# Pooled attention and two expert layers on one core: the first token block's layers in three float32r products instead of plain float32

## The chip, the cores and the metric

The kernel runs on one NeuronCore of a Trainium2 chip. The metric is the time of one execution on the device in microseconds (us). The engines are named as in the profile: PE is TensorE (PEld its weight loads), DVE is VectorE, ACT is ScalarE, POOL is GpSimd, SP is the queue that issues all DMAs of this kernel.

## The reference

Inputs are q, k and v (8 batches, 8 heads, 576 tokens, 64 features, float32), and the matrices w_a, w_b, w_out of a first layer and w_in, w_out of a second, which come as float64.

```python
k_p = k.reshape(B, H, Sp, pool, D).mean(axis=3)      # pool = 8, Sp = 72
v_p = v.reshape(B, H, Sp, pool, D).mean(axis=3)
scores = scale * np.matmul(q, k_p.transpose(0, 1, 3, 2))
...                                                  # softmax over the 72 pooled keys
x = np.matmul(attn, v_p)                             # 4608 tokens x 512
y = (x @ w_a) * (x @ w_b) @ w_out                    # 512 -> 1536 -> 512
h = y @ w_in                                         # 512 -> 2048
out = (h * np.clip(h + 3.0, 0.0, 6.0) / 6.0) @ w_out2
```

## The kernel before

The 4608 tokens are cut into nine blocks of 512. For each block j, attention gives x (512 features in four groups of 128 partitions, by 512 tokens), and the first layer runs over twelve slices f of 128 hidden features. `step(j, f)` (L646) issues for a slice: the product pa of x with a slice of w_a, the product pb with a slice of w_b, their elementwise product g, and, one step late (`pend`), `y_part` (L513), which adds w_out times g to the four accumulators of the block. At the end of a block y goes to DRAM. After all blocks the second layer runs over the whole of y; the change does not touch it.

**Two ways of multiplying.** From block 1 on, each operand is split into a float32r high half and a float32r low half (`split`, L72: the high half is a rounding copy, by default on ScalarE; the low half is a subtraction, by default on GpSimd), and a product takes three matmuls, high by high, low by high and high by low (`mm3`, L495; recorded at L497, L498 and L499). In block 0 x, the weights and g are left whole, and the products are plain float32 (L505 and L519).

**The decode.** The weights are float64, read as pairs of 32-bit words, and each tile (128 by 512 weights, 512 KB, named st) is turned into float32 in block 0, in three stages: `decode_begin` (two operations on ScalarE, L79 and L80), `decode` (two on VectorE, L85 and L86, and an add on GpSimd, L87) and `decode_end` (one on VectorE, L91). A slice f has three tiles, part 0 (w_a), 1 (w_b) and 2 (w_out), numbered n = 3 f + part. A step is cut into three slots, s = 3 f, 3 f + 1 and 3 f + 2 in block 0; `run_slot(s)` issues the attention work that is planned for the slot, `w1_slot(s)` (L468) issues begin of tile s + 4, end of tile s + 2 and mid of tile s + 3. Everything is issued in the order of the program (`manual_schedule`), and each engine works through its own instructions in order.

**The splits of the weights.** They are made from the last step of block 0 on, one step ahead: `wa_split` (L474) of the w_a slice, whose tile then stays in SBUF for all later blocks, and `raw_split` (L484) of the other two, which are also stored to DRAM (`w1dram`) in the next step. From block 2 on, `w1_load` reads these two back three steps ahead. Staged, raw, split and loaded tiles share the 28 buffers of `wpool`.

**The plan of the attention.** The tokens of a block fall into chunks of up to 128. `plan` gives every piece of work of a chunk a slot: q transposed (`q_tr`), scores, exponential (`expo`), sums, normalisation (`normal`, three operations on GpSimd, L296, L303, L309), transposes of the attention (`at_main`, `at_left`), the product with v (`pv`, which also writes x into `xh`, and from block 1 on the low half into `xl`, L360). For a new batch, k and v are summed over 8 (`sum8`, L132 to L134), and their loads are issued some slots earlier (`dma_at`, L406), into four buffers of the pool `ld` for batches 1 and 2.

**The prelude** (L576) does this for block 0 by a list written by hand. It loads k of the first head pair, q of chunk 0, the other k, q of chunk 1, v, the last rows of v (`vl`), q of chunks 2 and 3 and the first nine weight tiles. `sc(c)` transposes q of a chunk and takes its scores at once.

```python
        def sc(c):
            q_tr(c)
            scores(c, 0)
            scores(c, 1)
```

Of the kernel before, what the change touches and what calls it, by code (L numbers as in the profile page):

```python
# [15 lines left out]

# [9 lines left out]
def pooled_attention_then_two_moe_kernel(  # L26
# [79 lines left out]
    def x_tiles(j):  # L106
        if j not in xh_t:
            xh_t[j] = xpool.tile([P, NCC, TB], F32R if j else F32, tag="xh", name=f"xh{j}")
            xl_t[j] = xpool.tile([P, NCC, TB], F32R, tag="xl", name=f"xl{j}") if j else None
        return xh_t[j], xl_t[j]  # L110
# [77 lines left out]
    def vl_prep(b):  # L188
        t = vlraw.pop(b)
        vs = a2.tile([96, 2, D], F32, tag="kv", name="vls", bufs=3)  # L190
        sum8(vs, t)
        vpool[b, 2] = vs
# [152 lines left out]
    def pv(pi, g):  # L345
        b, t0, N = pieces[pi]
        ath, atl, atx = aT[pi]
        pt = ps.tile([P, 2, PIECE], F32, tag="att", name="pv")
        for i in range(2):
            hp = 2 * g + i  # L350
            o = pt[:, i, :N]
            nc.tensor.matmul(o, vmh[b % 2][:, hp], ath[:, hp, :N], start=True, stop=False)
            nc.tensor.matmul(o, vml[b % 2][:, hp], ath[:, hp, :N], start=False, stop=False)
            nc.tensor.matmul(o, vlw[b % 2][:96, hp], atx[:, g, :N], start=False, stop=False)
            nc.tensor.matmul(o, vmh[b % 2][:, hp], atl[:, hp, :N], start=False, stop=True)
        j, r = divmod(b * S + t0, TB)
        xh, xl = (x[:, 2 * g : 2 * g + 2, r : r + N] if x is not None else x for x in x_tiles(j))
# [80 lines left out]
    wa_t, raw_t, rawa_t, w1st, wst = {}, {}, {}, {}, {}  # L438
# [10 lines left out]

    def w1_begin(n):  # L450

        f, part = divmod(n, 3)
        if part == 0:
            raw_t[f] = wpool.tile([P, 2, 512], F32, tag="w", name=f"raw{f}")
            if f % 2 == 0:
                rawa_t[f] = wpool.tile([P, 2, 512], F32, tag="w", name=f"rawa{f}")
            else:
                rawa_t[f] = rawa_t[f - 1]
        wst[n] = raw_t[f][:, part - 1] if part else rawa_t[f][:, f % 2], w1st[f][part]
        decode_begin(*wst[n])  # L460
# [4 lines left out]
    def w1_end(n):  # L465
        decode_end(*wst.pop(n))
# [7 lines left out]
    def wa_split(f):  # L474
        w = wpool.tile([P, 2, 512], F32R, tag="w", name=f"wa{f}")
        split(w[:, 0], w[:, 1], rawa_t[f][:, f % 2], lo_eng=nc.vector)
        wa_t[f] = w
# [5 lines left out]

    def raw_split(key, f, part):  # L484
        w = wpool.tile([P, 2, 512], F32R, tag="w", name=f"sp{key}_{part}")
        split(w[:, 0], w[:, 1], raw_t[f][:, part], lo_eng=nc.vector if part else nc.gpsimd)
        later.append((w1dram[f][part], w.bitcast(F32)))
        sp_t[key, part] = w
# [12 lines left out]
    def layer_in(o, w, xh, xl):  # L501
        for c in range(NCC):
            s = slice(c * P, (c + 1) * P)
            if xl is None:
                nc.tensor.matmul(o, w[:, s], xh[:, c], start=c == 0, stop=c == NCC - 1)  # L505
                continue
# [6 lines left out]
    def y_part(j, f, w, gh, gl):  # L513
        if f == 0:
            yacc[j] = [ps_acc.tile([P, TB], F32, tag="acc", name=f"y{c}") for c in range(NCC)]
        for c in range(NCC):
            s = slice(c * P, (c + 1) * P)
            if gl is None:
                nc.tensor.matmul(yacc[j][c], w[:, s], gh, start=f == 0, stop=f == NF1 - 1)  # L519
                continue  # L520
# [55 lines left out]
    def prelude():  # L576

        k_dma(0, 0)
        q_dma(0)
        for hp in range(1, NP):  # L580
            k_dma(0, hp)
# [3 lines left out]
        vl_dma(0)  # L585
        q_dma(2)
        q_dma(3)
        for f in range(3):
            w1_dma(f)
# [4 lines left out]
        def sc(c):  # L594
            q_tr(c)
            scores(c, 0)
            scores(c, 1)
# [4 lines left out]

        sc(0)
# [3 lines left out]
        sums(0)  # L607
        v_prep(0, 1)
        expo(1)
        normal(0)  # L610
        v_write(0, 0)
        sums(1)
        sc(2)
        w1_begin(0)
        normal(1)
        at_chunk(0)
        expo(2)
        vl_prep(0)
        v_write(0, 1)
        sums(2)  # L620
        w1_mid(0)
        sc(3)
        normal(2)
        expo(3)
        vl_split(0)
        at_chunk(1)
        w1_begin(1)
        w1_end(0)
        sums(3)
# [12 lines left out]
        w1_begin(3)
# [3 lines left out]
    def step(j, f):  # L646
# [11 lines left out]
        nj, nf = divmod(NF1 * j + f + 1, NF1)  # L658
# [10 lines left out]
        layer_in(pa, wa_t[f] if j else rawa_t[f][:, f % 2], xh, xl)  # L669
# [60 lines left out]
    t = 0  # L730
# [228 lines left out]
```

## Time and profile before

| | us |
|---|---|
| median of three runs | 1855.4 |
| lowest and highest | 1855.19, 1856.17 |
| the profiled execution | 1853.53 |
| its span | 1851.7 |

The profile is of one execution. Times in it count from the start of the span. A row of a timeline gives start, duration, engine, line, operation, output and input; a row of groups gives line, engine, operation, output and input, shapes and count, then the busy time and the mean duration in ns, then the idle time of the engine just before and what ended it. Matmuls overlap in the records, so the price of one is read from start to start.

### The profile page before, as it was taken

The numbers are of one execution on the slowest core, as the hardware profiler recorded it, in microseconds if no ns is written. First come the engines' busy times: TensorE is split into PE (matmuls) and PEld (weight loads), VectorE is DVE, ScalarE is ACT, GpSimd is POOL, SyncE is SP. The second block draws the span as 40 slices with busy tenths as digits, with TensorE's granted clock in tenths as the row PEclk, the third lists the DMA queues.
The fourth block names the chain that finished last, engine by engine and source line by source line (L and its number), as shares of the span: only waits on it lengthen the run. The fifth ranks groups of instructions, "written<-read, shape, count | busy, mean of one in ns | idle before, by whom it ended". The sixth has DMA issues, their size and how long they took to land.

```text
span 1851.7 us, 23399 instructions
## 1 busy us (share of the span) xinstructions
PE 1796.2 (97%) x8148; PEld 1438.6 (78%) x8148; DVE 947.3 (51%) x1609; ACT 726.9 (39%) x1389; POOL 763.0 (41%) x661
## 2 busy tenths in 40 slices
PE   4999999999999999999999989999999999999998
PEld 3444788888888788888888777888888888888897
DVE  6687655323444445444322336676557445644645
ACT  3544443323333333333333335444334433533443
POOL 3454454333443444444343575554225222422322
PEclk8999999999999999999999999999999999999999
DMA  9552346635746547565545465546445544644483
GB/s 250 174 161 50 115 145 214 217 109 154 247 150 195 199 150 229 183 210 185 187 160 199 163 244 185 207 173 227 151 151 182 178 146 142 210 137 149 152 296 127
DMA packets 196549, 328.72 MB, mean 178 GB/s; under 512 B 86352, under 2 KB 107856, under 8 KB 196432
## 3 DMA queue, kind: packets, MB, share of 16 engines
q1 hardware_dynamic: 196432, 327.22, 53.5%
q8 instruction: 65, 1.06, 0.2%
q14 instruction: 52, 0.43, 0.1%
HBM read 264.24 MB, written 62.91 MB: 177 GB/s over the span
## 4 chain that ended last, share of the span: by engine, by line
PE 88%; DVE 5%; DMA 1%; ACT 1%; issue 1%; POOL 0%; SPq 0%; DVEq 0%; ACTq 0%; POOLq 0%
PE o L497 7%; PE o L499 7%; PE o L498 7%; PE y L497 5%; PE pb L497 5%; PE y L499 4%; PE pb L499 4%; PE y L498 4%; PE pb L498 4%; PE pa L497 4%; PE pa L499 4%; PE pa L498 4%; PE phZ L497 3%; PE phZ L498 3%; PE phZ L499 3%; PE sc L258 2%
## 5 line engine op out<-in xcount | busy, mean ns | idle before, releaser
L74 POOL TENSOR_TENSOR g<-r,g 128x512 fp32r<-128x512 f32 (+1 forms) x160 | 198.3, 1249 | 433.4 <-ACT g L73 263.8
L847 DVE TENSOR_TENSOR oacc<-o,oacc 128x512 f32<-128x512 f32 x252 | 172.2, 688 | 135.7 <-PE o L499 135.5
L498 PE MATMUL o<-wo,g 128*128 128x512 f32 x576 | 224.4, 390 | 0.0
L499 PE MATMUL o<-wo,g 128*128 128x512 f32 x576 | 224.2, 389 | 0.0
L689 POOL TENSOR_TENSOR asb<-asb,bsb 128x512 f32<-128x512 f32 x96 | 126.9, 1322 | 232.1 <-ACT bsb L684 206.8
L497 PE MATMUL o<-wo,g 128*128 128x512 f32 x576 | 211.6, 390 | 1.4 <-ACT g L73 1.2
L74 POOL TENSOR_TENSOR gl<-asb,gh 128x512 fp32r<-128x512 f32 x96 | 126.8, 1321 | 146.3 <-ACT gh L73 144.1
L671 ACT COPY asb<-pa 128x512 f32<-128x512 f32 x108 | 63.3, 586 | 243.0 <-PE pa L499 207.1
L497 PE MATMUL pa<-xh,wa 128*128 128x512 f32 x384 | 154.7, 403 | 0.0
L499 PE MATMUL pa<-xl,wa 128*128 128x512 f32 x384 | 150.2, 391 | 0.0
L498 PE MATMUL pa<-xh,wa 128*128 128x512 f32 x384 | 149.7, 390 | 0.0
L684 ACT COPY bsb<-pb 128x512 f32<-128x512 f32 x108 | 63.3, 586 | 192.4 <-PE pb L499 160.7
L828 ACT ACTIVATE r<-hs 128x512 f32<-128x512 f32 (+1 forms) x120 | 69.0, 590 | 164.7 <-DVE hs L878 163.8
L497 PEld LDWEIGHTS o<-wo,g 128*128 128x128 f32 x576 | 107.5, 188 | 23.8 <-ACT g L73 2.4
L499 PEld LDWEIGHTS o<-wo,g 128*128 128x128 f32 x576 | 108.1, 188 | 22.2
L498 PEld LDWEIGHTS o<-wo,g 128*128 128x128 f32 x576 | 108.2, 188 | 22.0
L73 ACT CAST g<-r 128x512 fp32r<-128x512 f32 (+1 forms) x160 | 91.9, 579 | 68.4 <-DVE r L829 68.2
L498 PE MATMUL phZ<-Sh,wi 128*128 128x512 f32 (+1 forms) x320 | 117.7, 368 | 0.0
L497 PE MATMUL phZ<-Sh,wi 128*128 128x512 f32 (+1 forms) x320 | 117.6, 368 | 0.0
L499 PE MATMUL phZ<-Sl,wi 128*128 128x512 f32 (+1 forms) x320 | 114.6, 368 | 0.0
L331 DVE TENSOR_TENSOR atl<-atm,ath 128x512 fp32r<-128x512 f32 (+1 forms) x40 | 25.5, 637 | 165.6 <-ACT ath L330 165.5
L829 DVE SCALAR_TENSOR_TENSOR r<-r,hs 128x512 f32<-128x512 f32 (+1 forms) x120 | 95.0, 808 | 26.5 <-ACT r L828 26.4
(1349 smaller groups left out, 4216.3 us busy)
## 6 DMA issues: line engine op xcount, KB each, us to landing
wi<-wsd SPq DMA_DIRECT2D x96, 512.0 KB
wo<-wod SPq DMA_DIRECT2D x64, 512.0 KB
wsd<-wi SPq DMA_DIRECT2D x24, 512.0 KB
kraw<-in_k_dram SPq DMA_DIRECT2D x32, 288.0 KB
ydram<-yo SPq DMA_DIRECT2D x36, 256.0 KB
out_dram<-oacc SPq DMA_DIRECT2D x36, 256.0 KB
vraw<-in_v_dram SPq DMA_DIRECT2D x32, 256.0 KB
w2st<-in_moe_w_in_dram SPq DMA_DIRECT2D x16, 512.0 KB
```

The source lines that it names most:

```text
L73: (hi_eng or nc.scalar.copy)(hi, src)
L74: (lo_eng or nc.gpsimd).tensor_tensor(lo, src, hi.bitcast(F32), ALU.subtract)
L258: nc.tensor.matmul(pt[:n, i * 2 * SP : (i + 1) * 2 * SP], qT[c][:, hp, :], bd[b % 2][hp], start=True, stop=True)
L497: nc.tensor.matmul(o, wh, xh, start=first, stop=False, skip_group_check=more)
L498: nc.tensor.matmul(o, wl, xh, start=False, stop=False, skip_group_check=more)
L499: nc.tensor.matmul(o, wh, xl, start=False, stop=last, skip_group_check=more)
L671: nc.scalar.copy(asb, pa)
L684: nc.scalar.copy(bsb, pb)
L689: nc.gpsimd.tensor_tensor(asb, asb, bsb, ALU.mult)
L828: nc.scalar.activation(r[:, :n], src, AF.Relu, bias=3.0)
L829: nc.vector.scalar_tensor_tensor(r[:, :n], r[:, :n], 6.0, src, ALU.min, ALU.mult)
L847: nc.vector.tensor_tensor(acc, o, acc, ALU.add)
```

## The change

Block 0 is computed like the others: x, weights and g are split, and every product takes three matmuls. Each tile of weights is decoded and split in block 0, one tile per slot: `w1_slot` now has four stages, begin of tile s + 5, mid of s + 4, end of s + 3 and split of s + 2; a stage may do two tiles in a slot until it has caught up, and takes only tiles that the stage before it had done when the slot began. High halves go to ScalarE, low halves to VectorE for parts 0 and 2 and to GpSimd for part 1. Parts 1 and 2 are stored to DRAM from block 0 on, and block 1 loads them, as the later blocks do. The splits in the last step of block 0 and in block 1 go away. The raw tiles come in pairs that are freed after the splits. In the prelude, all k are loaded before q of chunk 0, and the last rows of v after q of all chunks; q of a chunk is transposed about one chunk before its scores; the sum of those last rows moves from VectorE to GpSimd; tiles 0 and 1 are split. For batch 2, k is loaded three slots before its sum instead of six.

```diff
 def x_tiles(j):
-            xh_t[j] = xpool.tile([P, NCC, TB], F32R if j else F32, tag="xh", name=f"xh{j}")
-            xl_t[j] = xpool.tile([P, NCC, TB], F32R, tag="xl", name=f"xl{j}") if j else None
+            xh_t[j] = xpool.tile([P, NCC, TB], F32R, tag="xh", name=f"xh{j}")
+            xl_t[j] = xpool.tile([P, NCC, TB], F32R, tag="xl", name=f"xl{j}")
 def vl_prep(b):
-        sum8(vs, t)
+        sum8(vs, t, nc.vector if b else nc.gpsimd)
 def pv(pi, g):
         nc.scalar.copy(xh, pt[:, :, :N])
-        if j:
-            nc.vector.tensor_tensor(xl, pt[:, :, :N], xh.bitcast(F32), ALU.subtract)
+        nc.vector.tensor_tensor(xl, pt[:, :, :N], xh.bitcast(F32), ALU.subtract)
...
-            dma_at = [x - (6 if near else 8) for x in k_at], [x - (7 if near else 8) for x in v_at]
+            dma_at = [x - (3 if b == 2 else 6 if near else 8) for x in k_at], [x - (7 if near else 8) for x in v_at]
...
     def w1_begin(n):
...
+        if n % 2 == 0:
+            raw_t[0] = wpool.tile([P, 2, 512], F32, tag="w", name=f"raw{n}")
+        wst[n] = raw_t[0][:, n % 2], w1st[f][part]
         decode_begin(*wst[n])
...
+    def w1_split(n):
+        f, part = divmod(n, 3)
+        t, _ = wst.pop(n)
+        w = wpool.tile([P, 2, 512], F32R, tag="w", name=f"w1_{n}")
+        split(w[:, 0], w[:, 1], t, lo_eng=nc.gpsimd if part == 1 else nc.vector)
+        if part == 0:
+            wa_t[f] = w
+        else:
+            later.append((w1dram[f][part - 1], w.bitcast(F32)))
+            sp_t[(0, f), part - 1] = w
+
+    w1_done = [0] * 4
     def w1_slot(s):
-        for lead, fn in ((4, w1_begin), (2, w1_end), (3, w1_mid)):
-            if s + lead < 3 * NF1:
-                fn(s + lead)
+        limit = w1_done[1:] + [3 * NF1]
+        for i, (lead, fn) in enumerate(((2, w1_split), (3, w1_end), (4, w1_mid), (5, w1_begin))):
+            for _ in range(2):
+                if w1_done[i] <= s + lead and w1_done[i] < limit[i]:
+                    fn(w1_done[i])
+                    w1_done[i] += 1
...
 def prelude():
-        k_dma(0, 0)
+        for hp in range(NP):
+            k_dma(0, hp)
         q_dma(0)
-        for hp in range(1, NP):
-            k_dma(0, hp)
         q_dma(1)
         v_dma(0, 0)
         v_dma(0, 1)
-        vl_dma(0)
         q_dma(2)
         q_dma(3)
+        vl_dma(0)
...
 def step(j, f):
-        if nj == 1:
-            wa_split(nf)
-            raw_split((nj, nf), nf, 0)
-        if 2 <= lj < NB:
+        if 1 <= lj < NB:
             w1_load((lj, lf), lf, 0)
             w1_load((lj, lf), lf, 1)
...
-        if j == 0:
-            gh = gpool.tile([P, TB], F32, tag="gh", name="g0")
-            nc.gpsimd.tensor_tensor(gh, asb, bsb, ALU.mult)
-        else:
-            nc.gpsimd.tensor_tensor(asb, asb, bsb, ALU.mult)
+        nc.gpsimd.tensor_tensor(asb, asb, bsb, ALU.mult)
...
         gh = gpool.tile([P, TB], F32R, tag="gh", name="gh")
         gl = gpool.tile([P, TB], F32R, tag="gl", name="gl")
         split(gh, gl, asb)
```

## Rows read from the trace of the kernel before

**Rows 1.** The page: busy time of each engine over the span.

```profile
PE 1796.2 (97%) x8148; PEld 1438.6 (78%) x8148; DVE 947.3 (51%) x1609; ACT 726.9 (39%) x1389; POOL 763.0 (41%) x661
```

**Rows 2.** Stretches: from:to, length, busy per engine (instructions), PEclk, DMA share, GB/s.

```profile
10.00:49.60 39.60, 23.06 (x106) 20.10 (x107) 25.45 (x58) 16.85 (x39) 15.29 (x21) 0.74 1.02 274
49.60:194.30 144.70, 139.41 (x411) 67.02 (x410) 110.79 (x217) 69.12 (x140) 71.80 (x62) 0.98 0.42 119
194.30:208.20 13.90, 13.90 (x51) 8.54 (x50) 5.23 (x10) 5.27 (x10) 5.36 (x6) 1.00 0.26 102
208.20:330.00 121.80, 120.68 (x584) 100.30 (x584) 67.36 (x114) 53.24 (x109) 59.47 (x49) 1.00 0.54 178
```

**Rows 3.** Timeline of TensorE, in block 0 and in block 1.

```profile
162.69 3.60 PE L505 MATMUL pb<-xh,raw 128*128 128x512 f32 x8
166.12 3.60 PE L519 MATMUL y<-g,raw 128*128 128x512 f32 x8
...
172.41 0.38 PE L150 MATMUL ktp<-ident,kp 72*128 72x72 f32 x1 [1.61 <-DVE atl L331]
172.58 5.27 PE L505 MATMUL pa<-xh,rawa 128*128 128x512 f32 x8
...
218.96 0.39 PE L497 MATMUL pa<-xh,wa 128*128 128x512 f32 x1
...
221.68 0.39 PE L497 MATMUL pb<-xh,sp(1, 2)_0_1674 128*128 128x512 f32 x1
```

**Rows 4.** Groups of instructions: 49.6 to 194.3 us, the last over the whole span.

```profile
L87 POOL TENSOR_TENSOR raw<-raw,st 128x512 int32<-128x512 int32 x23 | 30.3, 1316 | 42.7 <-DVE raw L86 30.2 <-issue 10.4 <-DMA qraw<-in_q_dram 2.1
L87 POOL TENSOR_TENSOR rawa<-rawa,st 128x512 int32<-128x512 int32 x11 | 15.2, 1378 | 25.8 <-issue 12.1 <-ACT bsb L684 5.4 <-ACT st L80 4.1
L91 DVE SCALAR_TENSOR_TENSOR raw<-st,raw 128x512 uint32<-128x512 uint32 x23 | 18.8, 817 | 11.7 <-POOL raw L87 11.7
L91 DVE SCALAR_TENSOR_TENSOR rawa<-st,rawa 128x512 uint32<-128x512 uint32 x11 | 9.0, 814 | 0.5 <-POOL rawa L87 0.5
...
L74 POOL TENSOR_TENSOR gl<-asb,gh 128x512 fp32r<-128x512 f32 x96 | 126.8, 1321 | 146.3 <-ACT gh L73 144.1
```

**Rows 5.** Timeline of VectorE and of GpSimd at two places of block 0.

```profile
59.91 0.69 DVE L91 SCALAR_TENSOR_TENSOR raw<-st,raw 128x512 uint32<-128x512 uint32 x1 [2.91 <-POOL raw L87]
60.52 0.42 DVE L85 TENSOR_SCALAR raw<-raw 128x512 f32<-128x512 f32 x1
...
66.86 1.45 POOL L687 TENSOR_TENSOR g<-asb,bsb 128x512 f32<-128x512 f32 x1
67.29 1.17 DVE L134 TENSOR_TENSOR kp<-kraw 72x128 f32<-72x128 f32 x1
68.39 0.68 DVE L91 SCALAR_TENSOR_TENSOR rawa<-st,rawa 128x512 uint32<-128x512 uint32 x1
...
130.52 1.29 POOL L87 TENSOR_TENSOR rawa<-rawa,st 128x512 int32<-128x512 int32 x1 [3.27 <-ACT bsb L684]
131.78 1.26 POOL L687 TENSOR_TENSOR g<-asb,bsb 128x512 f32<-128x512 f32 x1
131.84 1.75 DVE L91 SCALAR_TENSOR_TENSOR rawa<-st,rawa 128x512 uint32<-128x512 uint32 x1 [0.48 <-POOL rawa L87]
133.01 1.48 POOL L296 TENSOR_TENSOR am<-sm,rc 128x512 f32<-128x512 f32 x1
133.52 1.26 DVE L85 TENSOR_SCALAR raw<-raw 128x512 f32<-128x512 f32 x1
```

**Rows 6.** Timeline of GpSimd in the prelude: the first and last of a normalisation's three operations.

```profile
39.45 1.04 POOL L296 TENSOR_TENSOR am<-sm,rc 128x512 f32<-128x512 f32 x1 [3.44 <-DVE rc L283]
...
40.83 0.34 POOL L309 COPY am<-ln 128x192 f32<-128x192 f32 x1
```

**Rows 7.** Waits of SP's queue up to 300 us: in total, times, longest.

```profile
SPq L223 <- DVE vs L134: 26.6, 1, 26.6
```

**Rows 8.** Groups of TensorE in the prelude, 0 to 49.6 us.

```profile
L258 PE MATMUL sc<-bd,qT 128*128 128x144 f32 x32 | 7.1, 382 | 6.9 <-ACT qT L241 6.9
```

More of the change, by code (lines that the diff above doesn't have):

```diff
@@ L356, in pv @@
         j, r = divmod(b * S + t0, TB)
-        xh, xl = (x[:, 2 * g : 2 * g + 2, r : r + N] if x is not None else x for x in x_tiles(j))
+        xh, xl = (x[:, 2 * g : 2 * g + 2, r : r + N] for x in x_tiles(j))
         nc.scalar.copy(xh, pt[:, :, :N])
-        if j:
-            nc.vector.tensor_tensor(xl, pt[:, :, :N], xh.bitcast(F32), ALU.subtract)
+        nc.vector.tensor_tensor(xl, pt[:, :, :N], xh.bitcast(F32), ALU.subtract)
     chunks, pieces, chunk_piece, block_chunks = [], [], {}, [[] for _ in range(NB)]
@@ L435, in run_slot @@
             fn(*args)
-    wa_t, raw_t, rawa_t, w1st, wst = {}, {}, {}, {}, {}
+    wa_t, raw_t, w1st, wst = {}, {}, {}, {}
     def w1_dma(f):
@@ L452, in w1_begin @@
         f, part = divmod(n, 3)
[L453 to L456, printed above, removed]
-            else:
-                rawa_t[f] = rawa_t[f - 1]
-        wst[n] = raw_t[f][:, part - 1] if part else rawa_t[f][:, f % 2], w1st[f][part]
+        if n % 2 == 0:
+            raw_t[0] = wpool.tile([P, 2, 512], F32, tag="w", name=f"raw{n}")
+        wst[n] = raw_t[0][:, n % 2], w1st[f][part]
         decode_begin(*wst[n])
@@ L465, in w1_end @@
     def w1_end(n):
-        decode_end(*wst.pop(n))
-    def w1_slot(s):
-        for lead, fn in ((4, w1_begin), (2, w1_end), (3, w1_mid)):
-            if s + lead < 3 * NF1:
-                fn(s + lead)
[L474 to L477, printed above, removed]
+        decode_end(*wst[n])
+    def w1_split(n):
[9 more added lines that the diff above has]
+    w1_done = [0] * 4
+    def w1_slot(s):
+        limit = w1_done[1:] + [3 * NF1]
[4 more added lines that the diff above has]
+                    w1_done[i] += 1
     sp_t = {}
@@ L482, in pooled_attention_then_two_moe_kernel @@
     w1dram = [[dpool.tile([P, 2, 512], F32, name=f"w1dram{f}_{i}") for i in range(2)] for f in range(NF1)]
[L484 to L488, printed above, removed]
     def w1_load(key, f, part):
@@ L503, in layer_in @@
             s = slice(c * P, (c + 1) * P)
-            if xl is None:
-                nc.tensor.matmul(o, w[:, s], xh[:, c], start=c == 0, stop=c == NCC - 1)
-                continue
             mm3(o, w[:, 0, s], w[:, 1, s], xh[:, c], xl[:, c], c == 0, c == NCC - 1)
@@ L517, in y_part @@
             s = slice(c * P, (c + 1) * P)
-            if gl is None:
-                nc.tensor.matmul(yacc[j][c], w[:, s], gh, start=f == 0, stop=f == NF1 - 1)
-                continue
             mm3(yacc[j][c], w[:, 0, s], w[:, 1, s], gh, gl, f == 0, f == NF1 - 1)
@@ L594, in sc @@
         def sc(c):
-            q_tr(c)
             scores(c, 0)
@@ L601, in at_chunk, with w1 @@
             at_left(c)
+        def w1(stage, n):
+            (w1_split, w1_end, w1_mid, w1_begin)[stage](n)
+            w1_done[stage] = n + 1
+        q_tr(0)
+        q_tr(1)
         sc(0)
@@ L607, in prelude @@
         sums(0)
+        q_tr(2)
+        expo(1)
         v_prep(0, 1)
-        expo(1)
         normal(0)
-        v_write(0, 0)
+        sc(2)
         sums(1)
-        sc(2)
-        w1_begin(0)
+        q_tr(3)
+        expo(2)
         normal(1)
         at_chunk(0)
-        expo(2)
+        v_write(0, 0)
+        sc(3)
+        sums(2)
+        expo(3)
         vl_prep(0)
+        w1(3, 0)
+        normal(2)
+        at_chunk(1)
         v_write(0, 1)
[L620 to L624, printed above, removed]
+        sums(3)
         vl_split(0)
[L626 to L629, printed above, removed]
+        w1(2, 0)
         vl_write(0)
         normal(3)
+        w1(3, 1)
         pv(0, 0)
         pv(0, 1)
+        w1(1, 0)
         at_chunk(2)
-        w1_mid(1)
-        w1_begin(2)
+        w1(2, 1)
+        w1(0, 0)
+        w1(3, 2)
         at_chunk(3)
-        w1_end(1)
+        w1(1, 1)
         pv(1, 0)
         pv(1, 1)
-        w1_mid(2)
-        w1_begin(3)
+        w1(2, 2)
+        w1(0, 1)
+        w1(3, 3)
         for x in sorted(x for x in plan if x < 0):
@@ L657, in step @@
                 w1_dma(f + 3)
-        nj, nf = divmod(NF1 * j + f + 1, NF1)
-        if nj == 1:
-            wa_split(nf)
-            raw_split((nj, nf), nf, 0)
         lj, lf = divmod(NF1 * j + f + AHEAD, NF1)
-        if 2 <= lj < NB:
+        if 1 <= lj < NB:
             w1_load((lj, lf), lf, 0)
@@ L668, in step @@
         pa = ps.tile([P, TB], F32, tag="ab", name="pa")
-        layer_in(pa, wa_t[f] if j else rawa_t[f][:, f % 2], xh, xl)
+        layer_in(pa, wa_t[f], xh, xl)
         asb = gpool.tile([P, TB], F32, tag="asb", name="asb", bufs=2)
@@ L681, in step @@
         pb = ps.tile([P, TB], F32, tag="ab", name="pb")
-        layer_in(pb, sp_t.pop(((j, f), 0)) if j else raw_t[f][:, 0], xh, xl)
+        layer_in(pb, sp_t.pop(((j, f), 0)), xh, xl)
         bsb = gpool.tile([P, TB], F32, tag="bsb", name="bsb", bufs=1)
         nc.scalar.copy(bsb, pb)
-        if j == 0:
-            gh = gpool.tile([P, TB], F32, tag="gh", name="g0")
-            nc.gpsimd.tensor_tensor(gh, asb, bsb, ALU.mult)
-        else:
-            nc.gpsimd.tensor_tensor(asb, asb, bsb, ALU.mult)
+        nc.gpsimd.tensor_tensor(asb, asb, bsb, ALU.mult)
         run_slot(s0 + 1)
@@ L694, in step @@
             y_part(*pend)
-        if nj == 1:
-            raw_split((nj, nf), nf, 1)
         run_slot(s0 + 2)
@@ L699, in step @@
             w1_slot(s0 + 2)
-            pend = (j, f, raw_t[f][:, 1], gh, None)
-            return
         gh = gpool.tile([P, TB], F32R, tag="gh", name="gh")
```

## The prediction

> **What bounds the kernel now.** I read the page first, then the stretches, then TensorE's timeline, then the groups of VectorE and GpSimd in the stretch that the change rewrites, then single neighbours on those two engines. The page shows TensorE busy 97% of the span [rows 1]. The stretches show where that holds: from 208.2 us, where the second token block is under way, it is busy 120.68 of 121.8 us, so nothing that the change takes off the other engines there can pay more than 1.1 us. In the decode stretch, 49.6 to 194.3 us (from the first pa of block 0 to the last decode_end), it is busy 139.41 of 144.7; before it, from 10 to 49.6, only 23.06 of 39.6 at a granted clock of 0.74 [rows 2]. So the change acts in the prelude and in block 0.
>
> The timeline gives the two prices of a layer of TensorE (pa, pb or y of one f). In block 0 pb of plain float32 starts at 162.69 and the y after it at 166.12: 3.43 us. With three float32r products pa starts at 218.96 and pb at 221.68: 2.72 us [rows 3]. The change makes 36 layers cheaper by 0.71 us each, 25.6 us in all. What it pays for that lies on VectorE and GpSimd.
>
> **The price on VectorE and GpSimd.** In the decode stretch GpSimd runs 34 adds of the decode (L87) and VectorE 34 decode_end (L91) [rows 4]; by the code there are with them 11 products on GpSimd (L687, one per step) and on VectorE 34 pairs L85 and L86 and eleven sums over 8 (eight of k, three of v). A GpSimd operation of this shape takes 1.26 us from start to start when the next is waiting (130.52 to 131.78); I take 1.25.
>
> The two engines do not run side by side. L687 runs from 131.78 to 133.04. L91, a 0.68 us operation, starts at 131.84 and ends at 133.59, 0.55 after L687. The multiplication of the softmax, L296, meanwhile takes 1.48 us and ends at 134.49; L85, elsewhere 0.42 us (at 60.52), starts at 133.52 and ends at 134.78, 0.29 after it. Likewise L134 ends at 68.46, 0.15 after the L687 that ends at 68.31 [rows 5]. Each waits for the other's instruction to end, and VectorE then needs 0.55, 0.29 or 0.15 us. I call these its holds. I give L86 the 0.29 of L85, the same shape; no row shows L86 waiting, so its lower bound is 0.
>
> The Trainium skill, page "SBUF — State Buffer", section "Who interferes with whom", speaks against this change: whichever of GpSimd and a VectorE instruction with two SBUF inputs or in a two-port mode issues first gets the shared port pair for the whole instruction, and the other is fully blocked. The rows agree that it is exclusive, but not that VectorE's whole recorded span counts. With whole spans (1.53 us for the three decode operations, 0.68 for a subtraction, 1.40 for a sum over 8, 1.29 for GpSimd) the sum below would be 178 us instead of 154.5, an estimate.
>
> Now the sum of exclusive time in the decode stretch.
>
> - Before: GpSimd 46 operations (34 L87, 11 L687, one subtraction) at 1.25, 57.5, and five normalisations at 1.72 (39.45 to 41.17 [rows 6]), 8.6. VectorE 34 tiles at 0.29+0.29+0.55 = 1.13, 38.4; one subtraction 0.55; eleven sums over 8 at 0.55+0.29+0.15 = 0.99, 10.9. Together 116, 80% of 144.7 us.
> - Added on GpSimd: gl of float32r for f = 0 to 10 (11, the price of the gl group, 1.32 recorded with its waits [rows 4], 1.25 without) and the low halves of the pb weights, tiles 4, 7, ... 34 (11); less the one subtraction of before. 21 at 1.25 is 26.3.
> - Added on VectorE: the low halves of 23 tiles (tiles 0 and 1 are split in the prelude), less the one of before: 22 at 0.55 is 12.1.
> - After: 154.5 us.
>
> The engines cannot use all of it, since each also waits for ScalarE and TensorE. The densest place of the trace is the step in which VectorE's 13 instructions from 59.91 to 69.07 follow one another [rows 5]: three L91, two pairs L85 and L86, two sums over 8 (1.65+1.16+1.98 = 4.79) and three GpSimd operations (3.75), 8.54 of 9.16 us, 93%. I take 93%: 154.5/0.93 = 166 us against 144.7, **21.4 us longer**. Bounds: 100% gives 154.5 (+9.8), and 86%, about half way back to the 80% of before, 180 (+35). TensorE needs 139.4 less 34 layers at 0.71, about 115 us, and is hidden; its saving is not seen.
>
> **The other parts.** *After the decode* (194.3 to 208.2 [rows 2]) TensorE is busy throughout, and two of its layers become cheaper: -1.4. *ScalarE* gets 34 high halves and 12 gh at about 0.6, 28 us on 69.1 in the stretch, 97 of 166: hidden. *Block 1* gives back its splits and 22 stores and loads 18 tiles instead (six are loaded at the end of block 0); the row shows it full, so 0, at best -1.1.
>
> *Queues.* SP carries 24 stores and 24 loads of 512 KB, nearly all stores now in block 0, where DMA is busy 0.42 [rows 2]; some 15 MB more on the 17 MB that 119 GB/s moved give about 190 GB/s, and the prelude moved 274. Hidden. A store waits for its split, with the next weight loads and the q, k and v loads behind it. SP already waits up to 26.6 us for a buffer [rows 7] without holding TensorE; weights have four slots from issue to decode. The later issue of k for batch 2 takes one such wait out of SP's way. I take 0; what it costs without that cover is the third rival.
>
> *Prelude.* q transposed a chunk ahead can give at most the 6.9 us that the scores wait for qT [rows 8]. vl_prep moves from VectorE to GpSimd. Added are two splits (ScalarE 1.2, VectorE 0.7, GpSimd 1.3) and four xl subtractions (at most 2.8). DMA, at 1.02 with the same bytes to fetch [rows 2], is the floor. Bounds -6.9 and +4.5 (TensorE waiting for the last split and xl); what is saved early is mostly spent again before the first pa, so I take -1.
>
> **Sum:** +21.4 - 1.4 - 1 = +19. The profiled execution took 1853.5 us around a span of 1851.7; the median of the runs is 1855.4, 1.9 more. 1853.5 + 19 + 1.9 = 1874 us.
>
> **Rivals.**
>
> *TensorE sets block 0 (faster).* GpSimd's gl and the subtractions run in gaps, and the 25.6 us of the layers come out: 1855.4 - 25.6 - 1 = 1829. For it: TensorE was busy 139 of 144.7 us while the exclusive time already filled 80%. Against it: it decides only if the exclusive time of the stretch stays below TensorE's 115 us, and GpSimd alone needs 92, VectorE's holds 62. Something of it (waits overlapping better than I count) gives 1829 to 1851. Chance 0.19.
>
> *A draw.* L86 takes no port (34 x 0.29 = 10 us less), the port is used fully: 144.6 us for 144.7, and the small terms cancel: 1852 to 1859. Chance 0.08. About 0.2%, 3.7 us, is what a measurement of this kernel tells from no change.
>
> *The stores and the buffers (much slower).* With a wa tile per step, three staged tiles, raw and split tiles, the 28 buffers of wpool are nearly used up from f = 7 on; a weight load waits for a buffer on SP with stores and attention loads behind it. Where five steps lose 4 us each, 20 us more: 1894 and above. For it: the waits of SP [rows 7]. Against it: weight loads are issued four slots ahead. Chance 0.05.
>
> *The clock.* A wait of 1.61 us (172.41) was followed by a pa of 5.27 us instead of 3.60 [rows 3]: 1.67 us. With TensorE busy some 70% of the stretch there will be several; most lie inside waits for weights. It is in the upper bound, not a case of its own.
>
> **How the numbers follow.** The forecast, the exclusive time of VectorE and GpSimd, has the chance 0.68. Its own range: +9.8 - 1.4 - 6.9 = +1.5, 1857, to +35 - 1.4 + 4.5 = +38, 1893. Reaching down over the draw and the nearest part of the faster rival, the range is 1846 to 1893; left out are most of that rival and the buffers, about 0.2. Slower by over 0.2%: 0.68 and 0.05, 0.73; the draw 0.08; faster 0.19.
>
> **What would show it.** In the changed trace: block 0's steps at 13 to 16 us although a layer takes 2.72; TensorE's waits before pb on L74's low halves and before y on gl, both of GpSimd; L91, L85 and the k sums with means well over 0.68, 0.42 and 0.7; GpSimd busy about 100 us in the decode stretch; the first pa within 3 us of 49.6 us; block 1 as long as before. The forecast is wrong if block 0 ends earlier than at 208 us counted from the same start, or if the loss lies in waits of SP or in a clock below 0.9 instead.

## The result, and the profile after

The changed kernel takes 1876.0 us (median of four runs, 1874.24 to 1878.94) where the kernel before takes 1855.3 in the same session: a ratio of 1.0112, interval 1.0095 to 1.013. It is slower by 20.7 us; the forecast was 19 (1874 us). The profiled execution is the slowest of the four, 1878.94 us around a span of 1876.8, so the traces differ by 25.1 us where the medians differ by 20.7.

The page of the changed kernel (beside [rows 1]):

```profile
PE 1787.1 (95%) x8292; PEld 1471.6 (78%) x8292; DVE 958.7 (51%) x1610; ACT 734.8 (39%) x1401; POOL 779.5 (42%) x676
```

TensorE works 9.1 us less and waits more. The stretches that answer to [rows 2]: the prelude up to the first pa, from there to the last low half of a decoded tile, to the second pa of block 1, and behind it. (Before, that second pa starts at 209.23, 1.0 us behind the third stretch of [rows 2].) Columns are from:to, length, busy per engine, clock, DMA share, GB/s.

```profile
10.00:45.80 35.80, 20.12 (x105) 17.32 (x106) 23.33 (x52) 16.83 (x37) 16.77 (x23) 0.79 0.99 259
45.80:219.40 173.60, 133.55 (x545) 100.45 (x545) 150.29 (x242) 93.43 (x184) 105.75 (x84) 0.89 0.61 190
219.40:232.80 13.40, 13.40 (x70) 11.25 (x68) 2.74 (x8) 4.00 (x9) 5.38 (x6) 1.00 0.74 228
232.80:330.00 97.20, 97.20 (x470) 81.42 (x470) 33.55 (x73) 28.78 (x58) 34.78 (x33) 1.00 0.52 160
```

The decode stretch is 173.6 us where it was 144.7: 28.9 longer. VectorE is now the busiest engine there (150.29 us, 87%), its waits inside instructions included. The first pa starts at 45.81 instead of 49.61, 3.8 earlier. The third pa of block 1 starts at 242.5 instead of 219.0, 23.5 later; 28.9 - 3.8 is 25.1, so the part between the decode and that pa is 1.6 shorter. Block 0 thus holds nearly all of the loss; what follows the third pa adds another 1.6 us in this execution (25.1 in the span less 23.5).

What TensorE waits for in the decode stretch (in total, times, longest):

```profile
PE pb L497 <- POOL w L73: 11.8, 9, 2.7
PE sc L257 <- DVE qT L244: 6.6, 4, 4.3
PE pa L497 <- DVE w L73: 5.9, 5, 4.4
...
PE y L498 <- POOL gl L73: 2.3, 3, 1.1
```

The groups that answer to [rows 4] and to the prices of the sum (lines are one or more lower than before: L86 is the decode's add, L90 its end, L85 its shift, L73 a low half):

```profile
L86 POOL TENSOR_TENSOR raw<-raw,st 128x512 int32<-128x512 int32 x34 | 47.9, 1410 | 64.8 <-DVE raw L85 49.7 <-issue 7.1 <-ACT raw L78 5.7
L73 POOL TENSOR_TENSOR gl<-asb,gh 128x512 fp32r<-128x512 f32 x11 | 15.7, 1423 | 0.0
...
L90 DVE SCALAR_TENSOR_TENSOR raw<-st,raw 128x512 uint32<-128x512 uint32 x34 | 39.4, 1161 | 10.0 <-POOL raw L86 9.4 <-DMA st<-in_moe_w_b_dram 0.6
L73 DVE TENSOR_TENSOR w<-raw,w 128x512 fp32r<-128x512 f32 x23 | 20.3, 882 | 5.2 <-ACT w L72 5.2
L85 DVE TENSOR_SCALAR raw<-raw 128x512 uint32<-128x512 uint32 x34 | 16.8, 493 | 1.2
```

L90 means 1161 ns instead of some 816: waiting for GpSimd is inside it. GpSimd in turn waits 49.7 us before L86 for VectorE's L85. One slot shows the ring, the chain of waits that leads from one L86 back to the next (timeline, VectorE and GpSimd):

```profile
79.64 1.32 POOL L86 TENSOR_TENSOR raw<-raw,st 128x512 int32<-128x512 int32 x1 [2.08 <-issue]
80.92 1.27 POOL L73 TENSOR_TENSOR w<-raw,w 128x512 fp32r<-128x512 f32 x1
80.99 1.75 DVE L90 SCALAR_TENSOR_TENSOR raw<-st,raw 128x512 uint32<-128x512 uint32 x1 [1.48 <-POOL raw L86]
82.67 0.41 DVE L84 TENSOR_SCALAR raw<-raw 128x512 f32<-128x512 f32 x1
83.11 0.43 DVE L85 TENSOR_SCALAR raw<-raw 128x512 uint32<-128x512 uint32 x1
83.62 1.68 POOL L86 TENSOR_TENSOR raw<-raw,st 128x512 int32<-128x512 int32 x1 [1.43 <-DVE raw L85]
```

L86 ends, GpSimd's next operation takes the port at once, L90 ends 0.55 us after that one, then come L84 and L85, and only then can the L86 of the next tile start: 3.98 us for this slot, 12 for a step of three such slots, whatever TensorE needs. It is one of the shortest; the slots of steps 2 to 4 take 3.95 to 5.10 us.

Where the 28 us of block 0 lie, by the start of the first pa matmul of each step, and how much of each stretch the shared port is held, by the prediction's own prices (number of operations times 1.25, 1.72, 0.29, 0.29, 0.55, and 0.99 for a sum over 8):

| steps of block 0 | before, us | held | after, us | held |
|---|---|---|---|---|
| 0 and 1 | 19.5 | 86% | 32.4 | 82% |
| 2 to 4 | 35.2 | 79% | 39.5 | 95% |
| 5 | 17.8 | 77% | 22.1 | 78% |
| 6 to 11 (held: to the end of the decode) | 76.6 | 80% | 83.1 | 95% |

### The profile page after: what moved, and what is told of

It is laid out like the page before. It is cut to its first block, busy times and chain, and to the rows that moved or that the text cites. A ratio compares the mean times of both kernels' runs of the same rounds, so it can differ in the third digit from the quotient of the medians.

```text
span 1876.8 us, 23793 instructions
## 1 busy us (share of the span) xinstructions
PE 1787.1 (95%) x8292; PEld 1471.6 (78%) x8292; DVE 958.7 (51%) x1610; ACT 734.8 (39%) x1401; POOL 779.5 (42%) x676
## 4 chain that ended last, share of the span: by engine, by line
PE 83%; DVE 7%; DMA 3%; POOL 3%; issue 2%; ACT 2%; SPq 1%; DVEq 0%; POOLq 0%; ACTq 0%
PE o L496 7%; PE o L497 7%; PE o L498 7%; PE pb L497 5%; PE pb L496 5%; PE pb L498 5%; PE y L496 5%; PE y L498 5%; PE y L497 5%; PE pa L496 4%; PE pa L498 4%; PE pa L497 4%; PE phZ L496 3%; PE phZ L497 3%; PE phZ L498 3%
## 5 line engine op out<-in xcount | busy, mean ns | idle before, releaser
L73 POOL TENSOR_TENSOR g<-r,g 128x512 fp32r<-128x512 f32 (+1 forms) x160 | 197.3, 1242 | 435.4 <-ACT g L72 264.8
L682 POOL TENSOR_TENSOR asb<-asb,bsb 128x512 f32<-128x512 f32 x108 | 144.1, 1334 | 255.3 <-ACT bsb L681 229.5
L73 POOL TENSOR_TENSOR gl<-asb,gh 128x512 fp32r<-128x512 f32 x108 | 144.1, 1334 | 146.5 <-ACT gh L72 145.0
L496 PE MATMUL pa<-xh,w 128*128 128x512 f32 x432 | 176.3, 408 | 2.6 <-ACT w L72 2.6
L497 PE MATMUL pa<-xh,w 128*128 128x512 f32 x432 | 171.1, 396 | 5.9 <-DVE w L73 5.9
L498 PE MATMUL pa<-xl,w 128*128 128x512 f32 x432 | 170.7, 395 | 0.0
L496 PE MATMUL phZ<-Sh,wi 128*128 128x512 f32 (+1 forms) x320 | 117.7, 368 | 0.0
L818 DVE SCALAR_TENSOR_TENSOR r<-r,hs 128x512 f32<-128x512 f32 (+1 forms) x120 | 94.1, 800 | 28.8 <-ACT r L817 28.7
```

The source lines that it names most:

```text
L73: (lo_eng or nc.gpsimd).tensor_tensor(lo, src, hi.bitcast(F32), ALU.subtract)
L496: nc.tensor.matmul(o, wh, xh, start=first, stop=False, skip_group_check=more)
L497: nc.tensor.matmul(o, wl, xh, start=False, stop=False, skip_group_check=more)
L498: nc.tensor.matmul(o, wh, xl, start=False, stop=last, skip_group_check=more)
L818: nc.vector.scalar_tensor_tensor(r[:, :n], r[:, :n], 6.0, src, ALU.min, ALU.mult)
```

## Experiments

The theory: the length of block 0 follows from the time in which GpSimd or VectorE holds the port. The rivals put it down to the start of block 0, to the stores, or to the order of issue.

For most runs two measures are given: the median of their times, and the length of block 0 in their one trace, from its first pa to the first pa of block 1 (149.1 us before, 177.1 in the changed kernel). They can differ by some 3 us, because the traces differ where no edit acts. From the last pa of the first layer to the end of the span, the changed kernel takes 760.0 us, and the runs on low halves, on all three parts and on later k sums take 762.6 to 762.9. Most of that is one wait of TensorE at the start of the second layer, here in the changed kernel and in the run on low halves (1080 to 1160 us):

```profile
PE phW L496 <- DVE hs L867: 4.4, 1, 4.4
```

```profile
PE phW L496 <- DVE hs L867: 6.4, 1, 6.4
```

**Low halves of part 1 on VectorE, alone.** In `w1_split`:

```diff
-        split(w[:, 0], w[:, 1], t, lo_eng=nc.gpsimd if part == 1 else nc.vector)
+        split(w[:, 0], w[:, 1], t, lo_eng=nc.vector)
```

> The changed kernel with the low halves of the pb weights (part 1) made on VectorE instead of GpSimd. Theory (exclusive time of the two engines): 11 operations cost 0.55 us of it instead of 1.25, 7.7 us less, at 89% use about 9 us faster than the changed kernel, 1867 us. Rival (VectorE is simply overloaded): 11 more operations of 0.6 us on it, about 7 us slower, 1883 us.

1873.3 us, ratio 1.0096 (1.0079 to 1.0113): 2.7 less than the changed kernel; the rival's slower time did not come. In the traces block 0 is 7.2 us shorter (169.9), 4.1 of it in steps 2 to 11; the theory counts 7.7 us of port time. The direction is the theory's; the size stays open between 2.7 and 7.2.

**Block 0's product on VectorE, alone.**

```diff
-        bsb = gpool.tile([P, TB], F32, tag="bsb", name="bsb", bufs=1)
-        nc.scalar.copy(bsb, pb)
-        nc.gpsimd.tensor_tensor(asb, asb, bsb, ALU.mult)
+        if j == 0:
+            nc.vector.tensor_tensor(asb, pb, asb, ALU.mult)
+        else:
+            bsb = gpool.tile([P, TB], F32, tag="bsb", name="bsb", bufs=1)
+            nc.scalar.copy(bsb, pb)
+            nc.gpsimd.tensor_tensor(asb, asb, bsb, ALU.mult)
```

> The changed kernel with the elementwise product of block 0 made on VectorE straight from PSUM, without the copy on ScalarE and the product on GpSimd. Theory: 12 GpSimd operations of 1.25 us leave the exclusive time, and VectorE's new operation has only one input in SBUF and takes none of it: 15 us less, at 89% use 17 us faster than the changed kernel, 1859 us. Rival (VectorE is overloaded): 12 more operations of 0.69 us on it, about 8 us slower, 1884 us.

1873.4 us, ratio 1.01 (1.0084 to 1.0115): 2.6 less, and 5.4 in block 0 (171.7). Both are far too small for the theory's 15 to 17.

**Both, and gl of block 0 on VectorE as well.**

```diff
-        split(gh, gl, asb)
+        split(gh, gl, asb, lo_eng=nc.vector if j == 0 else nc.gpsimd)
```

> Both edits before and the low half of g of block 0 on VectorE too, so that GpSimd keeps the adds of the decode and the normalisations. Theory: the exclusive time of the decode stretch falls from 154.5 to about 125 us, 141 us at 89% use, 33 us faster than the changed kernel, 1843 us, faster than the kernel before. Rival (VectorE is overloaded): some 22 us more work on it, 1898 us.

1863.1 us, ratio 1.0046 (1.0031 to 1.0061): 12.9 less, and 17.7 in block 0 (159.4): more than the two parts together, and about half of the 33 at most. (The third part, gl, has no run of its own.) Steps 2 to 4 take 31.9 us (39.5), steps 6 to 11 74.9 (83.1); steps 0 and 1 with 30.1 and step 5 with 22.4 stay. The stretches show why it stops there (steps 0 and 1, 2 to 4, 5, 6 to 10):

```profile
46.10:76.20 30.10, 20.35 (x65) 15.00 (x65) 22.37 (x40) 14.92 (x30) 8.37 (x6) 0.72 0.73 214
76.20:108.10 31.90, 30.03 (x137) 22.39 (x135) 30.17 (x56) 20.68 (x38) 14.37 (x12) 1.00 0.64 210
108.10:130.50 22.40, 16.11 (x66) 12.77 (x65) 21.67 (x45) 9.68 (x23) 7.41 (x7) 0.77 0.61 183
130.50:195.60 65.10, 54.45 (x255) 42.35 (x253) 63.21 (x127) 39.14 (x77) 28.84 (x24) 0.97 0.64 200
```

From step 2 on VectorE is busy 95% to 97%, what is left of its waits for GpSimd included: with half of GpSimd's operations gone it is the bound itself. It shows in a slot of the first experiment too. Taking GpSimd's second operation out of a slot leaves L86 waiting for a longer row of VectorE:

```profile
88.39 1.30 POOL L86 TENSOR_TENSOR raw<-raw,st 128x512 int32<-128x512 int32 x1 [1.42 <-DVE raw L85]
89.08 1.16 DVE L73 TENSOR_TENSOR w<-raw,w 128x512 fp32r<-128x512 f32 x1
...
91.21 0.43 DVE L85 TENSOR_SCALAR raw<-raw 128x512 uint32<-128x512 uint32 x1
91.78 1.63 POOL L86 TENSOR_TENSOR raw<-raw,st 128x512 int32<-128x512 int32 x1 [2.08 <-ACT w L72]
```

The second L86 starts 0.14 us after L85 ends; its row names ScalarE's copy, which had ended at 91.50. That slot takes 3.39 us where the same slot of the changed kernel takes 3.95 (92.40 to 96.35): 0.6 gained by removing 1.25, because a low half now stands in the ring itself, for about its price of 0.55. The operation was worth 1.25 less what took its place on VectorE.

**The decode's mid stage issued ahead of the end stage.** In `w1_slot` the order of the stages becomes split (2), mid (4), end (3), begin (5), with the leads in brackets, so that L86 of the next tile no longer waits for L90.

> The changed kernel with the decode's middle stage of a slot issued ahead of its end stage, so that the two operations on the next tile no longer stand behind decode_end, which waits for GpSimd. Theory (exclusive time): the sum of exclusive time is the same; only its use can rise from 89%, so 0 to 10 us faster, 1866 to 1876 us. Rival (a latency chain decode, add, decode_end, next decode through engines that wait in order): the chain is cut, at least 15 us faster, 1861 us or less.

1873.8 us, ratio 1.01 (1.0085 to 1.0116): 2.2 less, and 5.2 in block 0 (171.9), both within the theory's 0 to 10 and far from the rival's 15. The order of issue is not the main cause; steps 2 to 4 take 37.9 us instead of 39.5. The rows show why:

```profile
77.57 1.64 POOL L86 TENSOR_TENSOR raw<-raw,st 128x512 int32<-128x512 int32 x1 [1.48 <-PE ktp L149]
77.95 1.54 DVE L84 TENSOR_SCALAR raw<-raw 128x512 f32<-128x512 f32 x1
79.18 1.46 POOL L73 TENSOR_TENSOR w<-raw,w 128x512 fp32r<-128x512 f32 x1
79.53 1.39 DVE L85 TENSOR_SCALAR raw<-raw 128x512 uint32<-128x512 uint32 x1
81.00 1.70 POOL L86 TENSOR_TENSOR raw<-raw,st 128x512 int32<-128x512 int32 x1 [0.37 <-DVE raw L85]
```

GpSimd's wait before the second L86 falls from 1.43 to 0.37 us, but now L84 and L85 stand behind its operations, 1.54 and 1.39 us instead of 0.41 and 0.43, each ending 0.28 after one. The slot takes 3.43 us instead of 3.98.

**Only slice 0 stored.**

```diff
-            later.append((w1dram[f][part - 1], w.bitcast(F32)))
+            if f == 0:
+                later.append((w1dram[f][part - 1], w.bitcast(F32)))
...
-        nc.sync.dma_start(w.bitcast(F32), w1dram[f][part])
+        nc.sync.dma_start(w.bitcast(F32), w1dram[0][part])
```

> The changed kernel that stores only the split tiles of slice 0 to DRAM and lets later blocks read those for every slice, so that 22 stores are left out of block 0 (the later blocks compute with other weights). Theory (exclusive time): stores are no part of it, 0 to 2 us faster, 1874 to 1876 us. Rival (stores and buffers hold up SP's queue and the loads behind it): 10 to 20 us faster, 1856 to 1866 us.

1878.0 us, ratio 1.0118 (1.0103 to 1.0133): no gain. What SP waits for in front of the stores, from 45 to 235 us, in the changed kernel and then here:

```profile
SPq L675 <- POOL w L73: 72.4, 9, 13.2
```

```profile
SPq L676 <- POOL w L73: 12.8, 1, 12.8
```

The wait before the stores falls by 60 us and the time does not move. The queue as a whole does not wait less: all rows of SP together come to 116 us in the changed kernel and 129 here, now before loads (28.2 for the sum of v, 20.5 for a raw tile). In the changed kernel no wait of TensorE in the decode stretch ends with a DMA. So the stores are not the cause.

**The kernel before, with two more reading operations on GpSimd per step of block 0.**

```diff
+        if j == 0:
+            for _ in range(2):
+                spare = spool.tile([P, TB], F32, tag="wst", name="spare")
+                nc.gpsimd.tensor_tensor(spare, ident.unsqueeze(1).to_broadcast([P, 4, P]), ident.unsqueeze(1).to_broadcast([P, 4, P]), ALU.subtract)
```

> The kernel before with two more GpSimd subtractions in each step of block 0, that read SBUF and whose result nobody uses. Theory (exclusive time): 24 x 1.25 = 30 us more, 146 us in the decode stretch, 164 us at 89% use, 19 us slower than before, 1874 us. Rival (GpSimd, idle for half of the stretch, hides them): no change, 1855 us.

1866.7 us, ratio 1.0056 (1.0041 to 1.0071): some 11 more than before (block 0 is 9.5 longer), from operations whose results nothing waits for: far from the rival's 0, less than the 19 put down. The prediction's own sum gives it: 116 us held and 24 operations at 1.25, 30 us, make 146, at 93% 157 against 144.7, 12 longer. So the sum comes out where operations are added. The run does not tell the port from GpSimd's queue, though: the two operations also stand ahead of the next add, and L91 waits 18.8 us for it in the row below (50 to 200 us) instead of 11.7 [rows 4].

```profile
L91 DVE SCALAR_TENSOR_TENSOR raw<-st,raw 128x512 uint32<-128x512 uint32 x21 | 16.8, 802 | 18.8 <-POOL raw L87 18.8
```

**The kernel before, with five memsets on GpSimd per step instead.** The same place, `nc.gpsimd.memset(spare, 0.0)` five times.

> The kernel before with five GpSimd memsets in each step of block 0 instead of the two subtractions: as much time on GpSimd (about 0.5 us each by the memsets of the prelude), but nothing read. Theory (the two engines exclude each other where both read): the memsets hold up only VectorE's operations in a two-port mode, at most a third of the cost of the subtractions, 0 to 6 us slower than before, 1855 to 1861 us. Rival (GpSimd's own time or its place in the order is what counts): as slow as with the subtractions.

1864.7 us, ratio 1.0044 (1.0029 to 1.0059): 9 more, a miss of the theory's 0 to 6 and near to the rival's 11. Operations that read nothing cost nearly as much. The timeline shows whom they stop:

```profile
71.56 2.39 POOL L693 MEMSET spare<- 128x512 f32 x5
71.69 0.68 DVE L91 SCALAR_TENSOR_TENSOR rawa<-st,rawa 128x512 uint32<-128x512 uint32 x1
72.30 1.93 DVE L85 TENSOR_SCALAR raw<-raw 128x512 f32<-128x512 f32 x1
```

L91 runs beside the memsets in its usual 0.68 us. L85 (here the clamp of the decode) ends at 74.23, 0.28 after the last memset. Its groups from 50 to 200 us, in the kernel before and with memsets:

```profile
L85 DVE TENSOR_SCALAR raw<-raw 128x512 f32<-128x512 f32 x22 | 11.3, 514 | 0.0
```

```profile
L91 DVE SCALAR_TENSOR_TENSOR raw<-st,raw 128x512 uint32<-128x512 uint32 x22 | 17.4, 793 | 16.9 <-POOL raw L87 16.9
...
L85 DVE TENSOR_SCALAR raw<-raw 128x512 f32<-128x512 f32 x22 | 20.4, 925 | 0.5 <-ACT raw L79 0.5
```

L85 goes from 514 to 925 ns, 9 us in all; L91 on raw tiles, with two inputs from SBUF, stays at 793 (817 in [rows 4]). The Trainium skill, page "SBUF — State Buffer", section "Who interferes with whom", makes just this difference: an instruction in a two-port mode is kept out by any instruction of GpSimd, one with two inputs only by those that read. The rows agree; that the clamp runs in such a mode is concluded from its being held up. The rival has a share as well: L91 waits 16.9 us for the add instead of 11.7, since the memsets stand ahead of it in GpSimd's order.

**The kernel before with the new prelude alone** (q transposed a chunk ahead, the new order of loads, the sum of the last rows of v on GpSimd, batch 2's k loaded later).

> The kernel before with the change's prelude alone (loads of k first, q transposed a chunk ahead, the sum of v's last rows on GpSimd, the decode stages at their new places, without the splits) and the later load of k for batch 2. Theory: the prelude of the changed trace ended 3.8 us earlier, although it made two splits more; 4 us faster than before or a little more, 1850 to 1852 us. Rival (what is gained early is spent again before block 0 is through): no change, 1855 us.

1850.9 us, ratio 0.9972 (0.996 to 0.9985), faster than both kernels. The first pa starts at 42.5, 7.1 us earlier than before, and the steps of block 0 are as before. In the change 3.3 of the 7.1 are spent again; what was added there, the splits and the xl of the prelude, is the likely reason, but was not run alone.

**The k sums of batch 1 three slots later.** What stays in steps 0 and 1 after the third experiment looked like a late start. In the changed kernel the second step opens so:

```profile
57.51 0.50 PE L496 MATMUL pa<-xh,w 128*128 128x512 f32 x1 [2.59 <-ACT w L72]
62.37 0.79 PE L497 MATMUL pa<-xh,w 128*128 128x512 f32 x1 [4.36 <-DVE w L73]
62.96 0.63 PE L498 MATMUL pa<-xl,w 128*128 128x512 f32 x1
63.38 0.63 PE L496 MATMUL pa<-xh,w 128*128 128x512 f32 x1
```

On VectorE its low half (tile 3) is issued one slot ahead of its use, behind a k sum:

```profile
60.00 1.39 DVE L132 TENSOR_TENSOR kraw<-kraw 72x256 f32<-72x256 f32 x1
61.42 0.29 DVE L133 TENSOR_TENSOR kp<-kraw 72x128 f32<-72x128 f32 x1
61.63 0.68 DVE L73 TENSOR_TENSOR w<-raw,w 128x512 fp32r<-128x512 f32 x1
```

And TensorE, after waits of 2.59 and 4.36 us, runs at the lower of its two levels, 1.2 GHz (granted clock 0.50 from 62.9 to 67.2): 0.42 us from start to start (62.96 to 63.38). The edit:

```diff
-            k_at, v_at = [s0 - 9 + i for i in range(NP)], [s0 + 3 + i for i in range(3)]
-            dma_at = [x - (3 if b == 2 else 6 if near else 8) for x in k_at], [x - (7 if near else 8) for x in v_at]
+            k_at, v_at = [s0 - (6 if b == 1 else 9) + i for i in range(NP)], [s0 + 3 + i for i in range(3)]
+            dma_at = [x - (9 if b == 1 else 3 if b == 2 else 6 if near else 8) for x in k_at], [x - (7 if near else 8) for x in v_at]
```

> The changed kernel with one thing moved: the four k sums of batch 1 (VectorE, slots 1 to 4) and their writes stand three slots later; their loads stay where they are. Nothing is added or removed. Theory (steps 0 and 1 of block 0, 32.4 us together, are long because the low half of tile 3, which the second step's first layer waits for, is issued only one slot ahead and stands behind the k sums on VectorE): steps 0 and 1 take 25 to 29 us together, and the time falls by 3 to 8 us, to 1868 to 1873 us. Rival (the decode stretch is as long as the shared port's work in it, wherever the k sums stand): steps 0 and 1 shorten but the next steps lengthen by as much, and the time stays at 1874 to 1878 us.

1880.2 us, ratio 1.0133 (1.0115 to 1.0152): not faster. Steps 0 and 1 take 28.7 us, 3.7 less, and steps 2 to 4 take 42.6, 3.1 more, as the rival had it. In its trace block 1 starts 0.7 us earlier than in the changed kernel, and the stretch from the last pa of the first layer on, which the edit does not touch, takes 762.9 us instead of 760.0. So the 4.2 us that the median has on top cannot be put down to the edit.

**The decode one slot further ahead at the start of block 0.**

```diff
         w1(3, 3)
+        w1(1, 2)
+        w1(2, 3)
+        w1(3, 4)
+        w1(0, 2)
+        w1(1, 3)
+        w1(2, 4)
+        w1(3, 5)
```

> The changed kernel with the decoding one slot further ahead when block 0 begins: before it, tile 2 is ended and split, tile 3 decoded and ended, tile 4 begun and decoded, and tile 5 begun. Nothing else is changed. Theory (the splits of the first steps come too late because the decoding starts block 0 one slot short of its leads): the first step begins 1 to 3 us later than in the changed kernel (45.8 us), steps 0 and 1 take 22 to 27 us together instead of 32.4, and the time falls by 3 to 8 us, to 1868 to 1873 us. Rival (the port's work sets the end): what steps 0 and 1 lose is gained by the prelude and the later steps, and the time stays at 1874 to 1880 us.

1874.2 us, ratio 1.0099 (1.0083 to 1.0115): 1.8 less by the medians, 2.4 by the ratios, whose intervals overlap. Steps 0 and 1 take 28.5 us, 3.9 less, at a granted clock of 0.90 instead of 0.70; the first pa starts 0.9 later and steps 2 to 4 take 0.5 more. What is left, about 2.4 (block 1 starts 2.4 earlier in the trace), is less than the theory's 3 to 8.

**Both moves in the kernel of the third experiment.**

> Both moves together (k sums of batch 1 three slots later, decoding one slot further ahead at the start of block 0) in the kernel that has the low halves of block 0 and its product on VectorE. Theory (two separate costs, the shared port in every steady step and the late start in steps 0 and 1, so that their cures add up): steps 0 and 1 take 20 to 25 us together instead of 30.2, steps 2 to 4 stay near 32 us, and the time is 1863.1 less 5 to 10, 1853 to 1858 us, about the kernel before. Rival (one cost, the port's, which the earlier run has cured already): no further gain, 1861 to 1865 us.

1858.6 us, ratio 1.0013 (1.0004 to 1.0023): 4.5 less than the third experiment by the medians, 6 by the ratios (1.0046 less 1.0013), at the lower end of the theory's 5 to 10 and beyond the rival's 2. In the traces block 1 starts only 3.4 us earlier, between the two. Steps 0 and 1 fall to 22.3 us (30.1), but steps 2 to 4 rise to 36.1 (31.9) and steps 6 to 11 to 76.1 (74.9). So of the 7.8 us some 3.4 (traces) to 6 (ratios) are gained; the rest is work that the next steps do instead.

**The kernel before with the new prelude, and batch 1 loaded into wpool.** `load_tile` takes `wpool` if `b != 2`.

> The kernel before with the change's prelude, and with the loads of batch 1 (k, v, the last rows of v, and the q of its chunks) in buffers of wpool instead of the four of ld; nothing else is changed. Theory (the step of f = 5, 17.8 us in that kernel and 22.1 in the changed one, is long because the q of a chunk is loaded only when the sums over 8 of k and v have freed a buffer, so that the scores wait for a late qT): the step falls to 12 to 14 us, and the time from 1850.9 to 1845 to 1848 us. Rival (the step is long because the three sums of v and the decoding fill VectorE and GpSimd, and the buffers only follow them): the step stays within 1 us of 17.8, and the time at 1850 to 1852 us.

1850.6 us, ratio 0.9975 (0.9966 to 0.9985), as without the buffers, and the step of f = 5 stays at 17.8 us: the rival. Step 5 is a full VectorE, in which qT stands behind three sums of v and the decode; in the changed kernel it is the same (117.7 to 139.8, VectorE busy 21.41 of 22.1):

```profile
117.70:139.80 22.10, 15.14 (x66) 12.36 (x65) 21.41 (x40) 9.28 (x21) 10.09 (x10) 0.85 0.68 209
```

## Why the prediction was right, and where its terms were off

**The mechanism** was the one forecast: GpSimd and VectorE, which shut each other out, set the length of block 0, and TensorE's saving is not seen. Adding two reading operations per step to the kernel before costs 11 us, as the sum says; taking three of GpSimd's six operations out of each step (beside the normalisations) gives 13 back, 17.7 in block 0, where the sum said 33, since VectorE becomes the bound; stores (+2) and order (-2, 5.2 in block 0) matter little. The waits named in advance are there: pb on low halves of GpSimd (11.8 us), y on gl (2.3), L90 at 1.16 us. One is not: the clamp (L84, 0.50 us) is no longer than before. GpSimd is busy 105.75 us in the stretch, about 100 were named.

**The decode stretch: +28.9, forecast +21.4.** The amount of work was right: counted in the new trace it is 157.3 us by the same prices (154.5 forecast; a sixth normalisation falls into the longer stretch). The step that failed is "I take 93%" for the whole stretch. Steps 2 to 4 and 6 to 11 are held to 95%, but steps 0 and 1 to 82% and step 5 to 78%. At 93% these three would take 28.7 and 18.5 us instead of 32.4 and 22.1: 7.3 us. Over the stretch it is 91% (157.3 of 173.6): of the 7.5 us that the forecast was short, the added work makes 3.0 and the use 4.5. In step 5 VectorE is the bound with work that the sum left out (subtractions of v, reductions, transposes); in steps 0 and 1 the splits start late. So the forecast of even steps of 13 to 16 us was wrong: they run from 10.2 to 22.1.

The whole spans of the Trainium skill's page "SBUF — State Buffer" (section "Who interferes with whom") gave an estimate of 178 us, nearer to 173.6 than my 166, but not for its reason. In steps 2 to 4, 18 GpSimd operations, a normalisation and VectorE's whole spans (eight or nine tiles at 1.53, five low halves at 0.68, two parts of a k sum) would be some 42 us, an estimate from these rows, in a stretch of 39.5.

**The prelude: -3.8, forecast -1 (bounds -6.9 and +4.5).** "What is saved early is mostly spent again" was the wrong choice within the bounds: alone it gives 7.1 us, slightly past the bound of 6.9, which counted only the wait for qT. DMA was not the floor that the text took it for: up to the first pa that run too keeps DMA at 1.02, but fewer bytes are moved ahead of it (10 to 42.5 us at 268 GB/s, 8.7 MB, where 10.9 were moved from 10 to 49.6 before). The first pa was 3.8 us earlier, just outside the 3 named.

**After the decode: -1.6, forecast -1.4; queues and stores: 0,** as forecast. These misses partly cancel: +28.9 - 1.6 - 3.8 = 23.5 to the third pa of block 1, 25.1 in the span of an execution some 3 us above its median, and 20.7 in the medians. That 19 comes so close to 20.7 is in part luck.

**The rivals.** *TensorE sets block 0* fell: it waits. *A draw* needed L86 (now L85) free of the port. It is not: the L85 that starts at 57.97 takes 1.40 us and ends 0.29 after the add of GpSimd.

```profile
57.52 0.42 DVE L84 TENSOR_SCALAR raw<-raw 128x512 f32<-128x512 f32 x1
57.97 1.40 DVE L85 TENSOR_SCALAR raw<-raw 128x512 uint32<-128x512 uint32 x1
```

```profile
57.68 1.40 POOL L86 TENSOR_TENSOR raw<-raw,st 128x512 int32<-128x512 int32 x1 [2.02 <-DVE raw L85]
```

*Stores and buffers* fell with the run without stores. *The clock*: the text named a clock below 0.9 as a sign against it, and it is 0.89 over the stretch (0.70 in steps 0 and 1). The head start raised steps 0 and 1 to 0.90 and the time fell by some 2 us only. TensorE's busy time there fell from 21.45 to 17.61 us, by 3.8, as much as the two steps did, so inside them the run does not tell the clock from the late start. That the clock follows from TensorE's waits is what the rows suggest; no run tests it alone.

What stays open is a schedule that keeps the three products in block 0 and gains by them. The best tried is 2.4 us above the kernel before; the new prelude without them is some 5 below it.

## What to carry to other kernels

Before work is moved off TensorE, add up, stage by stage, the time in which GpSimd and VectorE shut each other out, and look at the ring of waits between them, not only at the busy shares: at 80% held, 25 us saved on TensorE became 21 lost. Use the density of each stage, not of the densest: steps full of other VectorE work stay far from it. Taking an operation out of such a ring gains its time less what moves into its place on the other engine, and a change made of several parts is worth running part by part: here one part alone was the faster kernel.

## What the runs showed of the hardware

Memsets of GpSimd, 0.54 us each, held up VectorE's clamp (514 to 925 ns) and left the two-input L91 on raw tiles as it was (817 and 793; 0.68 us beside five of them). VectorE also loses the port between two instructions that follow one another: in the rows above GpSimd's add is issued while L84 runs and comes in ahead of L85. The matmuls of the three products start 0.42 us apart after the wait of step 1 (62.96 and 63.38), at 1.2 GHz (granted clock 0.50), and 0.23 apart in the y that follows (75.92 and 76.15), at 2.4 (1.00 from 75.4 to 78.2).
